# Scales of queries, keys and values: row maxima summed over the partitions by a 12-column product with ones, in place of a maximum by diagonals

## The chip, the cores and the metric

The kernel runs on one core of a Trainium2 chip. The metric is the device time of one execution in microseconds (us), on that core. Engines are named as in the profile: PE is the matrix engine, PEld its weight loads, DVE the vector engine, ACT the scalar engine, POOL the general engine, SP the engine whose queue issues the transfers. Lines such as L110 are lines of the kernel before, unless the text says that they are of the changed kernel.

## The reference

Eight batches of twelve heads with 448 positions of 64 values are put through a sigmoid attention, and its output, 3584 tokens of 768 values, through a two-layer block with an ELU between the layers:

```python
scores = scale * np.matmul(q, k.transpose(0, 1, 3, 2)) - np.log(S)
attn = 1.0 / (1.0 + np.exp(-scores))
attn_out = np.matmul(attn, v)                      # 8, 12, 448, 64
x = attn_out.transpose(0, 2, 1, 3).reshape(B * S, H * D)
h = x @ w_in                                       # 768 x 2048
g = np.where(h > 0.0, h, np.exp(np.minimum(h, 0.0)) - 1.0)
return g @ w_out                                   # 2048 x 768
```

Queries, keys, values and results are float32; the two weight matrices come as float64.

## The kernel before, in words

Products are made of two float16 parts. A tensor is multiplied by a power of two and split into a high part (written by ACT) and what is left of it (written by DVE); a product is then high by high, low by high and high by low, three PE instructions that add up in one accumulator (`split`, L120). The powers of two are made on the chip, and this is what the change is about: a scale must be the same number on all 128 partitions, and it comes from the largest absolute value of a tensor.

**Pairs of heads.** The work on attention goes by 48 pairs (eight batches `b`, six pairs `hp`). For a pair, `raw` holds queries and keys (7 tiles of 128 positions; the fourth tile has the last 64 positions of the queries in its upper 64 partitions and those of the keys in its lower 64), `rv` the values. `prepare` (L294) makes three scales for a pair: for values, queries and keys. The six pairs of batch 0 need the scale of the values alone, since their scores are made in float32 (`EXACT = 1`); the 42 pairs of batches 1 to 7 need all three. DVE takes the maximum of `rv` (L125, tile `mx`, one column) and of the seven tiles of `raw` (L125, tile `mt`, seven columns), gathers the latter to one column for queries and one for keys (L307), and adds the mixed tile to both, on 64 partitions each (two instructions of L310). Then `magnitude` (L98) finds the maximum over the partitions:

- one `dg` per scale (L105): the 128 x 128 identity times the column of maxima, a diagonal,
- one PE product of ones with these diagonals (L110, tile `pb`, 128 columns for one scale, 384 for three), which puts the maxima of all partitions side by side on every partition,
- a DVE reduction (L112, tile `al`), a lower bound (L113), and the exponent bits (L114, tile `pw`).

After that DVE and POOL make the scales `sc` from `pw` (L318 to L324, L282 to L289), ACT and DVE split `raw` into `nat` and `rv` into `vn`, and a transfer transposes `nat` into `qk` (L352).

**Steps of a pair.** `scores` (L384, accumulator `psc`) gives score tiles; `soften` makes the sigmoid (L395) and, in batches 1 to 7, splits it (`at`, L413 on ACT, L414 on DVE); `values` (L433 and L425, accumulator `pav`) multiplies with the values; `finish` splits the result into `xh`, with a running scale over the pairs (`xs`). When a batch has its six pairs, `rescale` (L443) brings all of `xh` to one scale, whose maximum again goes through `magnitude`, with one diagonal.

**The two layers.** `moe1` (L479) runs 288 products a batch (L499, accumulator `ph`) with ELU on ACT and DVE behind each 18; `moe2` (L558) runs 48 products for each of its output tiles (L529, accumulators `po` and `po_r`). An odd batch of attention has 288 products of `moe2` of the batch before to interleave, an even one 384, because the last 64 positions of two batches share a tile.

**What sets the order.** Until the end of `moe1` of batch 0 a scheduler orders the instructions by a model of their times, among them the loads and splits of the weights. From batch 1 on (L685) PE, ACT, DVE and SP run in program order: for each pair first two tiles of scores, the rest of the preparation of the next pair (`third`), five or eight products groups of `moe2` (`fill`, three products each), then the maxima and diagonals of the pair after that (`prepare_pair`), two more tiles of scores, the rest of this pair's share of `moe2`, then the product L110 with what follows it (`second`), then `values` and `finish`. So on PE the product stands between the last `po` of a pair's share and the first `pav`. The last pair of a batch keeps four groups of `moe2` back until after `finish` (`tail`).

Of the kernel before, what the change touches and what calls it, by code (L numbers as in the profile page):

```python
# [23 lines left out]
TOP = 13  # L24
ATOP = 15
TINY = 2.0**-36
WTOP = 14
XTOP = 15
GTOP = 15
# [3 lines left out]
def attention_ffn(  # L33
# [9 lines left out]
    nc = tc.nc  # L43
    B, H, S, D = q.shape
    DM, DF = w_in.shape
    P = 128
    NP = H // 2
    NC = S // P
# [37 lines left out]
    stage, w_in_words = [], []  # L86
    ones = const.tile([P, P], BF16, name="ones")
    nc.vector.memset(ones, 1.0)
    eye = const.tile([P, P], BF16, name="eye")
    nc.vector.tensor_copy(eye, ident)  # L90

    rvs = []
    for i in range(2):
# [1 line left out]
        nc.gpsimd.memset(rv[:, 2 * NC :], 0.0)  # L95
        rvs.append(rv)

    def magnitude(dst, mx, n):  # L98

        dg = sb.tile([P, n, P], BF16, tag="dg", name="dg", bufs=2)
        for i in range(n):
            nc.vector.tensor_scalar(dg[:, i], eye, mx[:, i : i + 1], None, op0=ALU.mult)  # L105

        def rest():
            pb = ps.tile([P, 512], F32, tag="pm", name="pb", bufs=3)
            row = pb[:, : n * P].rearrange("p (n x) -> p n x", x=P)
            nc.tensor.matmul(row, ones, dg, start=True, stop=True)  # L110
            al = sb.tile([P, n], F32, tag="al", name="al", bufs=2)
            nc.vector.tensor_reduce(al, row, axis=AX.X, op=ALU.max)  # L112
            nc.vector.tensor_scalar(al, al, TINY, None, op0=ALU.max)  # L113
            nc.vector.tensor_scalar(  # L114
                dst.bitcast(U32), al.bitcast(U32), 0x7F800000, None, op0=ALU.bitwise_and
            )

        return rest

# [4 lines left out]
    def absmax(dst, src):  # L124
        nc.vector.tensor_reduce(dst, src, axis=AX.X, op=ALU.max, apply_absolute_value=True)  # L125
# [151 lines left out]
    def value_scale(b, hp, pv, c, xs):  # L277


        vm, vi = xs[:, 0], xs[:, 1]  # L280
        if hp:
            nc.vector.tensor_tensor(vm[:, hp : hp + 1], vm[:, hp - 1 : hp], pv, op=ALU.max)  # L282
        else:
            nc.gpsimd.tensor_copy(vm[:, 0:1], pv)
        nc.vector.reciprocal(vi[:, hp : hp + 1], vm[:, hp : hp + 1])
        if b < EXACT:
            nc.gpsimd.tensor_scalar(c, vi[:, hp : hp + 1], 2.0 ** (XTOP - 10), None, op0=ALU.mult)
        else:
            nc.gpsimd.tensor_scalar(  # L289
                c, vi[:, hp : hp + 1], pv, 2.0 ** (XTOP - 10 - TOP - ATOP),  # L290
                op0=ALU.mult, op1=ALU.mult,
            )

    def prepare(b, hp, raw, rv, xs):  # L294


        u = f"{b}_{hp}"
        n = 1 if b < EXACT else 3
        mx = sb.tile([P, 3], F32, tag="mx", name=f"mx{u}", bufs=2)
        absmax(mx[:, 0:1], rv.rearrange("p t d -> p (t d)"))  # L300
        if n > 1:
            mt = sb.tile([P, 2, NC + 1], F32, tag="mt", name=f"mt{u}", bufs=2)
            absmax(
                mt.rearrange("p i t -> p (i t)")[:, : 2 * NC + 1],
                raw.rearrange("p t h d -> p t (h d)"),
            )
            nc.vector.tensor_reduce(mx[:, 1:3], mt[:, :, :NC], axis=AX.X, op=ALU.max)  # L307
            for i, r in enumerate(rows):
                m = mx[r, 1 + i : 2 + i]
                nc.vector.tensor_tensor(m, m, mt[r, 0, NC:], op=ALU.max)  # L310
        pw = sb.tile([P, n], F32, tag="pw", name=f"pw{u}", bufs=2)
        product = magnitude(pw, mx[:, :n], n)

        def scales():
            product()
            sc = sb.tile([P, n + 3], F32, tag="sc", name=f"sc{u}", bufs=3)
            if b >= EXACT:
                nc.vector.reciprocal(sc[:, :n], pw)  # L318
                nc.gpsimd.tensor_scalar(sc[:, :n], sc[:, :n], 2.0**TOP, None, op0=ALU.mult)

                for i, r in enumerate(rows):
                    nc.gpsimd.tensor_copy(sc[r, n + 1 : n + 2], sc[r, 1 + i : 2 + i])

                nc.gpsimd.tensor_scalar(  # L324
                    sc[:, n + 2 :], pw[:, 1:2], pw[:, 2:3], 2.0 ** (-2 * TOP) / math.sqrt(D),
                    op0=ALU.mult, op1=ALU.mult,
                )
# [36 lines left out]

        return scales
# [77 lines left out]
    def rescale(b, xh, xs):  # L443


        vm, vi, xm = xs[:, 0], xs[:, 1], xs[:, 2]
        rr = sb.tile([P, NP + 3], F32, tag="rr", name=f"rr{b}", bufs=2)
        nc.vector.tensor_scalar(rr[:, :NP], vm, vi[:, NP - 1 :], None, op0=ALU.mult)
        for c in range(NP - 1):
            nc.vector.tensor_scalar(xh[:, c], xh[:, c], rr[:, c : c + 1], None, op0=ALU.mult)  # L450
        nc.vector.tensor_tensor(
            xm[:, : NP - 1], xm[:, : NP - 1], rr[:, : NP - 1], op=ALU.mult
        )
        yield
        mx, xp, xr = (rr[:, NP + i : NP + i + 1] for i in range(3))
        nc.vector.tensor_reduce(mx, xm, axis=AX.X, op=ALU.max)
        product = magnitude(xp, mx, 1)

        def rest():
            product()  # L460
            nc.vector.reciprocal(xr, xp)

        yield xp, xr, rest

    def moe_scales(m, xs, xr):

        vm, vi = xs[:, 0, NP - 1 :], xs[:, 1, NP - 1 :]
        nc.vector.tensor_scalar(
            m[:, 0], wp, vm, 2.0 ** (10 - XTOP - WTOP), op0=ALU.mult, op1=ALU.mult
        )  # L470

        nc.vector.tensor_scalar(
            m[:, 1], wr, vi, 2.0 ** (XTOP - 10 + GTOP - 2), op0=ALU.mult, op1=ALU.mult
        )
        nc.vector.tensor_scalar(m[:, 1], m[:, 1], xr, None, op0=ALU.mult)

# [69 lines left out]
    def out_scale(b, xs, xp, i=slice(0, NH)):  # L546
        if b % 2 == 0 and i.start == 0:
            oscs[0] = sb.tile([P, 3, NH], F32, tag="osc", name=f"osc{b}", bufs=2)
        j = b % 2
        o = oscs[0][:, j, i]  # L550
        nc.gpsimd.tensor_scalar(
            o, wop[:, i], wm[:, 0:1], 2.0 ** (10 - XTOP + 2 - GTOP - WTOP),
            op0=ALU.mult, op1=ALU.mult,
        )
        nc.gpsimd.tensor_scalar(o, o, xs[:, 0, NP - 1 :], xp, op0=ALU.mult, op1=ALU.mult)
        nc.gpsimd.tensor_copy(oscs[0][rows[j], 2, i], o[rows[j]])
# [206 lines left out]
```

## Time and profile before

| what | value |
|---|---|
| median of 3 runs | 1271.27 us |
| lowest and highest of the 3 | 1269.96 and 1274.96 us |
| span of the profiled execution, first to last instruction | 1269.1 us |
| PE busy | 1200.2 us, 95% of the span |
| DVE busy | 823.4 us, 65% |
| ACT busy | 671.8 us, 53% |
| product with diagonals, L110 | 56, of which 42 with 384 columns |
| diagonals, L105 | 140 instructions |
| reductions behind the product, L112 | 56 instructions, 27.2 us |

The time of the profiled execution is not listed apart from its span; the span is 0.9 us under the lowest of the three runs and 2.2 us under their median. A view of groups gives busy time, the mean of one in ns, and the idle time ahead of the group's instructions with what ended it. A line of the timeline has the start, the time from the first start to the last end, the engine and the group; consecutive instructions of a group are merged. PE instructions are pipelined, so their rows overlap: what one takes from the engine is the distance between two starts.

### The profile page before, as it was taken

The page shows a single profiled execution, that of the slowest core. Times are in us where ns is not written, and L with a number is a line of the kernel's source. Part 1 is how long each engine was busy: PE and PEld are TensorE (multiplying, and loading weights), DVE is VectorE, ACT ScalarE, POOL GpSimd, SP SyncE. Part 2 cuts the span into 40 slices and gives each one's busy share as a digit, 9 for nine tenths or more (in the row PEclk, how much of TensorE's full clock was granted, in tenths as well). Part 3 has the DMA queues.
Part 4 walks back from the last instruction along what each step waited for, and adds up shares of the span by engine and source line. Part 5 has one row for each costly group of instructions (what it writes and reads, how often), then busy time and mean ns, then how long its engine had stood idle before and what let it go on. Part 6 is the DMA issues. An engine that isn't in the chain of part 4 may idle for free.

```text
span 1269.1 us, 19337 instructions
## 1 busy us (share of the span) xinstructions
PE 1200.2 (95%) x7246; PEld 610.5 (48%) x7246; DVE 823.4 (65%) x1872; ACT 671.8 (53%) x1015; POOL 84.1 (7%) x319
## 2 busy tenths in 40 slices
PE   5979868999999999999999999999999999999998
PEld 2324334445555554545455554545455554455565
DVE  5898989765766557775666646885576656765500
ACT  5867777643655337744555436654565435663400
POOL 0011001100000000010000000010000100100000
PEclk9889979999999999999999999999999999999999
DMA  8937423420233103340144201440034401410000
GB/s 229 281 100 222 126 77 80 100 49 1 60 84 89 37 1 83 89 86 1 37 92 92 50 1 43 105 103 7 1 86 92 92 1 22 106 43 7 1 25 26
DMA packets 213407, 89.76 MB, mean 71 GB/s; under 512 B 177472, under 2 KB 209216, under 8 KB 213312
## 3 DMA queue, kind: packets, MB, share of 16 engines
q1 hardware_dynamic: 213312, 88.51, 28.7%
q8 instruction: 57, 0.93, 0.3%
q14 instruction: 38, 0.31, 0.1%
HBM read 58.20 MB, written 11.01 MB: 55 GB/s over the span
## 4 chain that ended last, share of the span: by engine, by line
PE 78%; ACT 8%; DVE 7%; DMA 3%; issue 2%; SPq 2%; DVEq 0%; POOL 0%; ACTq 0%; POOLq 0%
PE ph L499 31%; PE po L529 25%; PE psc L384 7%; PE pav L433 6%; PE po_r L529 5%; PE pav L425 3%; ACT sg L395 2%; DMA stage<-in_moe_w_in_dram 2%; ACT at L413 1%; SPq L262 1%; PE pb L110 1%; ACT L395 1%; ACT e L511 1%; DVE e L514 1%; DMA so<-in_moe_w_out_dram 1%
## 5 line engine op out<-in xcount | busy, mean ns | idle before, releaser
L499 PE MATMUL ph<-xh,wi 128*128 128x448 f16 x2304 | 442.0, 353 | 6.1 <-DVE xh L122 2.4
L529 PE MATMUL po<-wo,g 128*128 128x384 f16 x2304 | 392.9, 328 | 0.0
L529 PEld LDWEIGHTS <-g 128*128 128x128 f16 x2688 | 257.2, 98 | 198.4 <-issue 36.3
L499 PEld LDWEIGHTS <-wi 128*128 128x128 f16 x2304 | 225.3, 98 | 218.4 <-issue 7.6
L511 ACT ACTIVATE e<-ph,msc 128x448 f32<-128x448 f32 x128 | 80.8, 633 | 211.7 <-PE ph L499 211.6
L414 DVE SCALAR_TENSOR_TENSOR at<-sg,at 128x896 f16<-128x896 f32 x126 | 137.2, 1090 | 84.5 <-ACT at L413 84.5
L395 ACT ACTIVATE sg<-psc,bias,sc 128x896 f32<-128x896 f32 (+1 forms) x168 | 166.6, 992 | 1.7
L513 DVE TENSOR_SCALAR e<-e 128x448 f32<-128x448 f32 x128 | 50.3, 394 | 170.8 <-ACT e L511 170.7
L121 ACT ACTIVATE xh<-pav,sc 128x448 f16<-128x448 f32 x48 | 30.3, 632 | 216.7 <-PE pav L425 216.7
L384 PE MATMUL psc<-qk 64*128 64x448 f16 x1008 | 116.6, 355 | 11.4 <-ACT sg L395 11.4
L413 ACT ACTIVATE at<-sg 128x896 f16<-128x896 f32 x126 | 119.8, 951 | 4.1
L121 ACT ACTIVATE g<-e,msc 128x384 f16<-128x384 f32 (+1 forms) x192 | 96.0, 534 | 6.0 <-DVE e L514 4.3
L122 DVE SCALAR_TENSOR_TENSOR g<-e,msc,g 128x384 f16<-128x384 f32 (+1 forms) x192 | 94.6, 521 | 0.6
L514 DVE SCALAR_TENSOR_TENSOR e<-ph,msc,e 128x448 f32<-128x448 f32 x128 | 87.3, 683 | 4.0
L384 PEld LDWEIGHTS <-qk 64*128 64x128 f16 x1008 | 41.7, 97 | 89.7 <-issue 60.2
L433 PE MATMUL pav<-at,vn 128*64 128x448 f16 x756 | 80.2, 357 | 0.0
L324 POOL TENSOR_SCALAR sc<-pw 128x1 f32<-128x1 f32 x42 | 12.4, 295 | 843.5 <-DVE pw L114 790.9
L529 PE MATMUL po_r<-wo,g 128*128 128x384 f16 x384 | 64.7, 326 | 0.0
L122 DVE SCALAR_TENSOR_TENSOR xh<-pav,sc,xh 128x448 f16<-128x448 f32 x48 | 32.7, 680 | 48.7 <-ACT xh L121 48.7
L433 PEld LDWEIGHTS <-vn 128*64 128x64 f16 x756 | 39.4, 110 | 50.0 <-issue 27.8
L122 DVE SCALAR_TENSOR_TENSOR nat<-raw,sc,nat 128x384 f16<-128x384 f32 (+1 forms) x126 | 59.1, 524 | 0.0
L121 ACT ACTIVATE nat<-raw,sc 128x384 f16<-128x384 f32 (+1 forms) x126 | 58.8, 529 | 0.0
(103 smaller groups left out, 852.7 us busy)
## 6 DMA issues: line engine op xcount, KB each, us to landing
stage<-in_moe_w_in_dram SPq DMA_DIRECT2D x16, 768.0 KB, 6.6
raw<-in_q_dram SPq DMA_DIRECT2D x96, 96.0 KB, 3.1
raw<-in_k_dram SPq DMA_DIRECT2D x96, 96.0 KB, 2.6
rv<-in_v_dram SPq DMA_DIRECT2D x48, 192.0 KB, 2.7
out_dram<-o SPq DMA_DIRECT2D x48, 192.0 KB, 2.1
wo<-in_moe_w_out_dram SPq DMA_DIRECT2D x19, 384.0 KB, 4.1
so<-in_moe_w_out_dram SPq DMA_DIRECT2D x13, 384.0 KB, 4.3
raw<-in_q_dram SPq DMA_DIRECT2D x48, 32.0 KB, 2.4
```

Of the source, the lines that this page charges most:

```text
L121: nc.scalar.mul(hi, src, s)
L122: nc.vector.scalar_tensor_tensor(lo, src, s, hi, op0=ALU.mult, op1=ALU.subtract)
L384: nc.tensor.matmul(psc[:, j, :S] if g < NC else psc[rows[j], 0, :S], kk[rows[j], o], qq[rows[j], :S], start=(n == 0), stop=(n == len(parts ...
L395: a = nc.scalar.activation(sg[:, :nb], psc[:, :nb, :S], AF.Sigmoid, bias=bias, scale=self.s_scale)
L413: nc.scalar.mul(hi, sg, 2.0**ATOP)
L414: nc.vector.scalar_tensor_tensor(lo, sg, 2.0**ATOP, hi, op0=ALU.mult, op1=ALU.subtract)
L433: nc.tensor.matmul(pav[rows[j], :S], vv[i][:, j * NC + g], sg[k][:, j], start=(g == 0 and n == 0), stop=False,)
L499: nc.tensor.matmul(ph[:, :S], wi[:, wj, c, f * P : (f + 1) * P], xh[:, c, xj], start=(n == 0), stop=(n == 3 * NK - 1),)
L511: a = nc.scalar.activation(e, ph[:, :S], AF.Exp, scale=inv)
L513: nc.vector.tensor_scalar(e, e, 1.0, -1.0, op0=ALU.min, op1=ALU.add)
L514: nc.vector.scalar_tensor_tensor(e, ph[:, :S], inv, e, op0=ALU.mult, op1=ALU.max)
L529: nc.tensor.matmul(po[:, :HM], lh(gj, f), wo[:, i, f, wj], start=(n == 0), stop=(n == 3 * NF - 1),)
```

## The change

Instead of finding the maximum over the partitions, the kernel adds up over the partitions. DVE now writes maxima in bfloat16 into one tile `mx` of 15 columns, three groups of four with a gap: four for the values (`rv` is cut in four), three tiles each for queries and keys, and the mixed tile's maximum in both groups' last column, multiplied by a column that is one on its half of the partitions and zero on the other (`half`). PE multiplies ones with the 12 columns themselves (4 in batch 0), which puts the sum over the partitions of each column on every partition; DVE takes the largest of each four. The sum is an upper bound of the maximum, up to 128 times as large, so the constant for the running scale changes from 2^-10 to 2^-3 (`XBITS`). The maximum of `rescale` is still found by one diagonal, now made from the float32 identity (`greatest`); the bfloat16 copy of the identity is gone.

```diff
+    half = const.tile([P, 2], BF16, name="half")
+    nc.vector.memset(half, 0.0)
+    nc.vector.memset(half[:R, 0:1], 1.0)
+    nc.vector.memset(half[R:, 1:2], 1.0)
...
-    def magnitude(dst, mx, n):
-        dg = sb.tile([P, n, P], BF16, tag="dg", name="dg", bufs=2)
-        for i in range(n):
-            nc.vector.tensor_scalar(dg[:, i], eye, mx[:, i : i + 1], None, op0=ALU.mult)
+    def greatest(dst, mx):
+        dg = sb.tile([P, P], BF16, tag="dg", name="dg")
+        nc.vector.tensor_scalar(dg, ident, mx, None, op0=ALU.mult)
...
+    def sums_of_rows(dst, mx):
+        n = mx.shape[1]
         def rest():
-            pb = ps.tile([P, 512], F32, tag="pm", name="pb", bufs=3)
-            row = pb[:, : n * P].rearrange("p (n x) -> p n x", x=P)
-            nc.tensor.matmul(row, ones, dg, start=True, stop=True)
+            pb = ps.tile([P, 512], F32, tag="pm", name="pr", bufs=3)
+            sums = pb[:, : 4 * n].rearrange("p (n x) -> p n x", x=4)
+            nc.tensor.matmul(sums, ones, mx, start=True, stop=True)
             al = sb.tile([P, n], F32, tag="al", name="al", bufs=2)
-            nc.vector.tensor_reduce(al, row, axis=AX.X, op=ALU.max)
+            nc.vector.tensor_reduce(al, sums, axis=AX.X, op=ALU.max)
+            power_of_two(dst, al, TINY)
...
-        mx = sb.tile([P, 3], F32, tag="mx", name=f"mx{u}", bufs=2)
-        absmax(mx[:, 0:1], rv.rearrange("p t d -> p (t d)"))
+        mx = sb.tile([P, 15], BF16, tag="mx", name=f"mx{u}", bufs=2)
+        groups = mx.rearrange("p (n x) -> p n x", x=5)[:, :n, :4]
+        absmax(mx[:, 0:4], rv.rearrange("p (a t) d -> p a (t d)", a=4))
         if n > 1:
-            mt = sb.tile([P, 2, NC + 1], F32, tag="mt", name=f"mt{u}", bufs=2)
-            absmax(
-                mt.rearrange("p i t -> p (i t)")[:, : 2 * NC + 1],
-                raw.rearrange("p t h d -> p t (h d)"),
-            )
-            nc.vector.tensor_reduce(mx[:, 1:3], mt[:, :, :NC], axis=AX.X, op=ALU.max)
-            for i, r in enumerate(rows):
-                m = mx[r, 1 + i : 2 + i]
-                nc.vector.tensor_tensor(m, m, mt[r, 0, NC:], op=ALU.max)
+            absmax(mx[:, 6 : 2 * NC + 7], raw.rearrange("p t h d -> p t (h d)"))
+            nc.vector.tensor_tensor(
+                mx[:, 5:14:8], mx[:, 9:10].to_broadcast([P, 2]), half, op=ALU.mult
+            )
...
-            nc.gpsimd.tensor_scalar(c, vi[:, hp : hp + 1], 2.0 ** (XTOP - 10), None, op0=ALU.mult)
+            nc.gpsimd.tensor_scalar(c, vi[:, hp : hp + 1], 2.0 ** (XTOP - XBITS), None, op0=ALU.mult)
...
-        product = magnitude(xp, mx, 1)
+        product = greatest(xp, mx)
```

The order of the instructions shows three places. The first is DVE during pair 4 of batch 1, between the split of the next pair's values (`vn`) and the reduction behind the product; the digits in a name are the pair's number and a count. Before:

```order
L122 SCALAR_TENSOR_TENSOR vn_5_2351<-rv_85,sc_5_2286,vn_5_2351 128x384
L125 TENSOR_REDUCE mx_0_2384<-rv_83 128x1
L125 TENSOR_REDUCE mt_0_2386<-raw_0_2185 128x7
L307 TENSOR_REDUCE mx_0_2384<-mt_0_2386 128x2
L310 TENSOR_TENSOR mx_0_2384<-mx_0_2384,mt_0_2386 64x1 x2
L105 TENSOR_SCALAR dg<-eye,mx_0_2384 128x128 x3
L414 SCALAR_TENSOR_TENSOR at_4_2405<-sg_4_2403,at_4_2405 128x896
L537 TENSOR_SCALAR o_1_1_2450<-po_1_1_2366,osc_1613 128x384
L112 TENSOR_REDUCE al<-pb 128x3
```

And DVE at the same place of the changed kernel:

```order
L138 SCALAR_TENSOR_TENSOR vn_5_2299<-rv_87,sc_5_2234,vn_5_2299 128x384
L141 TENSOR_REDUCE mx_0_2332<-rv_85 128x4
L141 TENSOR_REDUCE mx_0_2332<-raw_0_2140 128x7
L321 TENSOR_TENSOR mx_0_2332<-mx_0_2332,half 128x2
L427 SCALAR_TENSOR_TENSOR at_4_2346<-sg_4_2344,at_4_2346 128x896
L550 TENSOR_SCALAR o_1_1_2391<-po_1_1_2314,osc_1589 128x384
L131 TENSOR_REDUCE al<-pr 128x3
```

Six instructions (L307, two of L310, three of L105) have become one (L321); the rest stands in the same order. The second place is PE where the product stands in the same pair, between `moe2` and `values`. Before:

```order
L529 LDWEIGHTS g
L529 MATMUL po_1_1_2366<-wo,g 128x384
L110 LDWEIGHTS ones
L110 MATMUL pb<-dg,ones 128x384
L433 LDWEIGHTS vn_4_2180
L433 MATMUL pav_4_2468<-at_4_2327,vn_4_2180 64x448
```

And PE in the changed kernel:

```order
L542 LDWEIGHTS g
L542 MATMUL po_1_1_2314<-wo,g 128x384
L129 LDWEIGHTS ones
L129 MATMUL pr<-mx_0_2332,ones 128x12
L446 LDWEIGHTS vn_4_2135
L446 MATMUL pav_4_2409<-at_4_2275,vn_4_2135 64x448
```

The product has 12 columns instead of 384 and stands at the same place. The third place is SP's queue in the part that the scheduler orders, around the loads of pair 0 of batch 1 (`raw_0`) and the loads of the first weight matrix (`stage`). Before:

```order
L266 DMA raw_5_521<-in_k_dram 64x2x64
L181 DMA stage<-in_moe_w_in_dram 128x6x128
L247 DMA rv_83<-in_v_dram 128x2x192
L262 DMA raw_0_649<-in_q_dram 128x3x64 x2
L252 DMA rv_83<-in_v_dram 64x64 x2
L266 DMA raw_0_649<-in_q_dram 64x2x64
L262 DMA raw_0_649<-in_k_dram 128x3x64 x2
L266 DMA raw_0_649<-in_k_dram 64x2x64
L181 DMA stage<-in_moe_w_in_dram 128x6x128 x3
```

And SP's queue in the changed kernel:

```order
L282 DMA raw_5_515<-in_k_dram 64x2x64
L197 DMA stage<-in_moe_w_in_dram 128x6x128 x3
L263 DMA rv_85<-in_v_dram 128x2x192
L278 DMA raw_0_641<-in_q_dram 128x3x64 x2
L282 DMA raw_0_641<-in_q_dram 64x2x64
L268 DMA rv_85<-in_v_dram 64x64 x2
L197 DMA stage<-in_moe_w_in_dram 128x6x128
L278 DMA raw_0_641<-in_k_dram 128x3x64 x2
L197 DMA stage<-in_moe_w_in_dram 128x6x128
L282 DMA raw_0_641<-in_k_dram 64x2x64
```

The loads of the weights have moved among the loads of queries, keys and values, some ahead and some back by a few places; PE, ACT and DVE are likewise reordered in the part that ends with `moe1` of batch 0 and the rest of the work on the second weight matrix: of that work ACT has 54 of 64 conversions and 12 of 32 splits ahead of its change from exponentials to sigmoids (at 162.9 us in the profile) before, and 58 and 16 now. From about 190 us on, the order differs only where instructions are gone or replaced.

More of the change, by code (lines that the diff above doesn't have):

```diff
@@ L26 @@
 TINY = 2.0**-36
+XTINY = 2.0**-24
+XBITS = 3
 WTOP = 14
@@ L88, in attention_ffn @@
     nc.vector.memset(ones, 1.0)
-    eye = const.tile([P, P], BF16, name="eye")
-    nc.vector.tensor_copy(eye, ident)
+    half = const.tile([P, 2], BF16, name="half")
+    nc.vector.memset(half, 0.0)
+    nc.vector.memset(half[:R, 0:1], 1.0)
+    nc.vector.memset(half[R:, 1:2], 1.0)
     rvs = []
@@ L96, in attention_ffn, with power_of_two, rest @@
         rvs.append(rv)
-    def magnitude(dst, mx, n):
-        dg = sb.tile([P, n, P], BF16, tag="dg", name="dg", bufs=2)
-        for i in range(n):
-            nc.vector.tensor_scalar(dg[:, i], eye, mx[:, i : i + 1], None, op0=ALU.mult)
+    def power_of_two(dst, al, tiny):
+        nc.vector.tensor_scalar(al, al, tiny, None, op0=ALU.max)
+        nc.vector.tensor_scalar(
+            dst.bitcast(U32), al.bitcast(U32), 0x7F800000, None, op0=ALU.bitwise_and
+        )
+    def greatest(dst, mx):
+        dg = sb.tile([P, P], BF16, tag="dg", name="dg")
+        nc.vector.tensor_scalar(dg, ident, mx, None, op0=ALU.mult)
         def rest():
             pb = ps.tile([P, 512], F32, tag="pm", name="pb", bufs=3)
-            row = pb[:, : n * P].rearrange("p (n x) -> p n x", x=P)
-            nc.tensor.matmul(row, ones, dg, start=True, stop=True)
-            al = sb.tile([P, n], F32, tag="al", name="al", bufs=2)
[L112 to L115, printed above, removed]
-            )
+            nc.tensor.matmul(pb[:, :P], ones, dg, start=True, stop=True)
+            al = sb.tile([P, 1], F32, tag="al", name="al", bufs=2)
+            nc.vector.tensor_reduce(al, pb[:, :P], axis=AX.X, op=ALU.max)
+            power_of_two(dst, al, XTINY)
+        return rest
+    def sums_of_rows(dst, mx):
+        n = mx.shape[1]
+        def rest():
+            pb = ps.tile([P, 512], F32, tag="pm", name="pr", bufs=3)
+            sums = pb[:, : 4 * n].rearrange("p (n x) -> p n x", x=4)
+            nc.tensor.matmul(sums, ones, mx, start=True, stop=True)
+            al = sb.tile([P, n], F32, tag="al", name="al", bufs=2)
+            nc.vector.tensor_reduce(al, sums, axis=AX.X, op=ALU.max)
+            power_of_two(dst, al, TINY)
         return rest
@@ L286, in value_scale @@
         if b < EXACT:
-            nc.gpsimd.tensor_scalar(c, vi[:, hp : hp + 1], 2.0 ** (XTOP - 10), None, op0=ALU.mult)
+            nc.gpsimd.tensor_scalar(c, vi[:, hp : hp + 1], 2.0 ** (XTOP - XBITS), None, op0=ALU.mult)
         else:
             nc.gpsimd.tensor_scalar(
-                c, vi[:, hp : hp + 1], pv, 2.0 ** (XTOP - 10 - TOP - ATOP),
+                c, vi[:, hp : hp + 1], pv, 2.0 ** (XTOP - XBITS - TOP - ATOP),
                 op0=ALU.mult, op1=ALU.mult,
@@ L298, in prepare @@
         n = 1 if b < EXACT else 3
-        mx = sb.tile([P, 3], F32, tag="mx", name=f"mx{u}", bufs=2)
-        absmax(mx[:, 0:1], rv.rearrange("p t d -> p (t d)"))
+        mx = sb.tile([P, 15], BF16, tag="mx", name=f"mx{u}", bufs=2)
+        groups = mx.rearrange("p (n x) -> p n x", x=5)[:, :n, :4]
+        absmax(mx[:, 0:4], rv.rearrange("p (a t) d -> p a (t d)", a=4))
         if n > 1:
-            mt = sb.tile([P, 2, NC + 1], F32, tag="mt", name=f"mt{u}", bufs=2)
-            absmax(
-                mt.rearrange("p i t -> p (i t)")[:, : 2 * NC + 1],
-                raw.rearrange("p t h d -> p t (h d)"),
-            )
-            nc.vector.tensor_reduce(mx[:, 1:3], mt[:, :, :NC], axis=AX.X, op=ALU.max)
-            for i, r in enumerate(rows):
-                m = mx[r, 1 + i : 2 + i]
-                nc.vector.tensor_tensor(m, m, mt[r, 0, NC:], op=ALU.max)
+            absmax(mx[:, 6 : 2 * NC + 7], raw.rearrange("p t h d -> p t (h d)"))
+            nc.vector.tensor_tensor(
+                mx[:, 5:14:8], mx[:, 9:10].to_broadcast([P, 2]), half, op=ALU.mult
+            )
         pw = sb.tile([P, n], F32, tag="pw", name=f"pw{u}", bufs=2)
-        product = magnitude(pw, mx[:, :n], n)
+        product = sums_of_rows(pw, groups)
         def scales():
@@ L468, in moe_scales @@
         nc.vector.tensor_scalar(
-            m[:, 0], wp, vm, 2.0 ** (10 - XTOP - WTOP), op0=ALU.mult, op1=ALU.mult
+            m[:, 0], wp, vm, 2.0 ** (XBITS - XTOP - WTOP), op0=ALU.mult, op1=ALU.mult
         )
         nc.vector.tensor_scalar(
-            m[:, 1], wr, vi, 2.0 ** (XTOP - 10 + GTOP - 2), op0=ALU.mult, op1=ALU.mult
+            m[:, 1], wr, vi, 2.0 ** (XTOP - XBITS + GTOP - 2), op0=ALU.mult, op1=ALU.mult
         )
@@ L551, in out_scale @@
         nc.gpsimd.tensor_scalar(
-            o, wop[:, i], wm[:, 0:1], 2.0 ** (10 - XTOP + 2 - GTOP - WTOP),
+            o, wop[:, i], wm[:, 0:1], 2.0 ** (XBITS - XTOP + 2 - GTOP - WTOP),
             op0=ALU.mult, op1=ALU.mult,
```

## The prediction

> **What bounds the kernel now.** I read the page's busy times first, then the busy times by stretch (below: stretch, its length, busy time of PE, PEld, DVE, ACT and POOL, PE clock, DMA share, GB/s), then PE's waits, and last the timeline around a few of the products that change.
>
> ```profile
> span 1269.1 us, 19337 instructions
> PE 1200.2 (95%) x7246; PEld 610.5 (48%) x7246; DVE 823.4 (65%) x1872; ACT 671.8 (53%) x1015; POOL 84.1 (7%) x319
> ...
> 0.00:60.00 60.00, 42.96 (x209) 17.84 (x211) 42.70 (x97) 40.12 (x52) 3.72 (x19) 0.94 0.91 249
> 60.00:153.00 93.00, 78.20 (x406) 35.70 (x405) 84.90 (x220) 66.34 (x113) 10.91 (x30) 0.96 0.50 153
> 153.00:200.00 47.00, 32.68 (x169) 15.07 (x169) 40.18 (x84) 38.02 (x65) 4.89 (x12) 0.80 0.31 88
> 200.00:1269.10 1069.10, 1046.32 (x6467) 541.89 (x6464) 655.60 (x1475) 527.33 (x788) 64.56 (x259) 1.00 0.24 53
> ```
>
> There are two kernels in one. Up to 60 us the DMA engines are 0.91 busy; from 60 to 200 us DVE leads (84.9 of 93, then 40.2 of 47 us). From 200 us on PE is busy for all but 22.8 us, and DVE for only 61%. So in the long part only two things count: time that a product takes on PE, and PE's waits. The latter are few:
>
> ```profile
> PE pb L110 <- DVE dg L105: 11.6, 6, 2.0
> PE psc L384 <- ACT sg L395: 6.7, 6, 1.2
> ```
>
> The largest wait from 200 us on is the very product that changes, six times for diagonals that DVE has not finished. One of the six, where an odd batch begins:
>
> ```profile
> 484.43 1.08 DVE L125 TENSOR_REDUCE mt<-raw 128x7 f32<-128x896 f32 x1
> ...
> 485.55 0.16 DVE L307 TENSOR_REDUCE mx<-mt 128x2 f32<-128x6 f32 x1
> 485.74 0.34 DVE L310 TENSOR_TENSOR mx<-mx,mt 64x1 f32<-64x1 f32 x2
> 486.11 0.58 DVE L105 TENSOR_SCALAR dg<-eye,mx 128x128 bf16<-128x128 bf16 x3
> 486.61 1.08 DVE L414 SCALAR_TENSOR_TENSOR at<-sg,at 128x896 f16<-128x896 f32 x1
> 486.75 0.32 PE L110 MATMUL pb<-dg,ones 128*128 128x384 bf16 x1 [1.97 <-DVE dg L105]
> ...
> 487.00 1.89 PE L433 MATMUL pav<-at,vn 128*64 128x448 f16 x18
> ```
>
> DVE runs without a break from the maxima to the diagonals, and PE starts 0.06 us after the third. PE stood still for 1.97 us; nothing else held it.
>
> **The change part by part.** The rows for what is removed, and for its nearest relatives:
>
> ```profile
> L125 DVE TENSOR_REDUCE mt<-raw 128x7 f32<-128x896 f32 x42 | 45.2, 1076 | 0.0
> L125 DVE TENSOR_REDUCE mx<-rv 128x1 f32<-128x512 f32 x48 | 32.6, 679 | 0.6 <-DMA rv<-in_v_dram 0.5 <-issue 0.2
> ...
> L105 DVE TENSOR_SCALAR dg<-eye,mx 128x128 bf16<-128x128 bf16 x132 | 26.1, 251 | 1.4
> L112 DVE TENSOR_REDUCE al<-pb 128x3 f32<-128x384 f32 x42 | 23.2, 551 | 15.2 <-PE pb L110 15.2
> L310 DVE TENSOR_TENSOR mx<-mx,mt 64x1 f32<-64x1 f32 x84 | 12.9, 154 | 2.7
> L307 DVE TENSOR_REDUCE mx<-mt 128x2 f32<-128x6 f32 x42 | 6.7, 159 | 1.3
> L112 DVE TENSOR_REDUCE al<-pb 128x1 f32<-128x128 f32 x14 | 4.0, 288 | 16.8 <-PE pb L110 16.8
> ```
>
> *The long waits.* From the start of L307 to the product it is 486.75 - 485.55 = 1.20 us. In its place stands one small instruction, 0.16 us by L307 and L310, and the same 0.06 us to PE: 0.22 us. So the product starts 0.98 us earlier, and six times that is 5.9 us. The two maxima ahead keep their price: their rows differ by 397 ns over 384 elements, about one ns an element, with seven results or with one, so I give nothing for four results instead of one. Were they slower by 0.1 us each, 1.2 us of the 5.9 would go; the other end is 11.6 us, were the waits to vanish. They will not: 1.97 - 0.98 leaves 0.99 us, because the chain ahead (sigmoid, split, `nat`, `vn`, the maxima) is not shortened. Behind the product PE needs the `at` of L414 only for its 17th and 18th `pav`; at 1.89 us for 18 these come some 1.6 us in, while that `at`, next in DVE's queue, ends within 1.1 us of the column. So no new wait appears there.
>
> *The short waits.* In odd batches most other products also stand behind their diagonals, for a moment that the view of waits does not show, since a product's row reaches into the next one's:
>
> ```profile
> 219.02 0.81 PE L529 MATMUL po<-wo,g 128*128 128x384 f16 x4
> 219.78 0.32 PE L110 MATMUL pb<-dg,ones 128*128 128x384 bf16 x1
> 220.03 0.38 PE L433 MATMUL pav<-at,vn 128*64 128x448 f16 x2
> ...
> 365.68 0.98 PE L529 MATMUL po_r<-wo,g 128*128 128x384 f16 x5
> 366.49 0.33 PE L110 MATMUL pb<-dg,ones 128*128 128x384 bf16 x1
> 366.75 0.57 PE L433 MATMUL pav<-at,vn 128*64 128x448 f16 x4
> ...
> 1117.11 0.81 PE L529 MATMUL po<-wo,g 128*128 128x384 f16 x4
> 1117.88 0.32 PE L110 MATMUL pb<-dg,ones 128*128 128x384 bf16 x1
> ```
>
> At 366.49 the product starts 0.17 us before the row of the `po` ends (366.66), at 219.78 only 0.05 us before (219.83): 0.12 us lost. From 219.78 to 1117.88 us, the first and the last shown, there are 14 such products; with a column that is ready 0.98 us earlier none should be left: 14 x 0.12 = 1.7 us.
>
> *The product itself.* What it takes from PE is the distance to the first `pav`: 0.26 us at 366.49, 0.25 us at 219.78. A product of 128 columns ahead of a `pav` is there once:
>
> ```profile
> 17.97 0.22 PE L110 MATMUL pb<-dg,ones 128*128 128x128 bf16 x1
> 18.11 0.60 PE L433 MATMUL pav<-sg,rv 128*64 128x448 f32 x2
> ```
>
> That is 0.14 us. So 256 columns cost 0.11 us, 0.43 ns each, and at 12 columns 0.14 - 116 x 0.43 ns = 0.09 us are left, which are the turn to the half-width weights of `pav` and stay. Saved: 0.16 us. How many there are, the reductions behind them (L112) say, of which 7 from 200 us on belong to `rescale`:
>
> ```profile
> 200.00:1269.10 1069.10, 23.55 (x46) 1.00 0.24 53
> ```
>
> So 39 of the 42 products lie behind 200 us: 39 x 0.16 = 6.2 us. This extrapolates below any row, so I bound it. At best all 0.16 us go; at worst a short product cannot follow its neighbours closer than the closest products with weights of their own do here:
>
> ```profile
> 52.30 0.51 PE L150 MATMUL si<-stage,ones 128*128 128x128 bf16 x6 [0.31 <-DVE al L112]
> ```
>
> Five distances and one row of 0.22 us make 0.51 us: 58 ns. Then the product takes 0.06 + 0.09 = 0.15 us and saves 0.10 us, 3.9 us in all. I take the upper value, since 58 ns is what 128 columns need at 0.43 ns (55 ns) and so shows no floor. [...]
>
> *The rest of DVE.* The reduction behind the product falls from 551 ns to 551 - 372 x 1.03 = 168 ns (slope from the two L112 rows), the three diagonals go, three small instructions become one: 0.75 + 0.38 + 0.31 = 1.4 us a pair. From 200 us on this beyond the waits is worth nothing: DVE is idle there for 39% of the time, and the scales behind it have time until `third`, on PE behind 18 `pav` (1.89 us above) and two tiles of scores. The diagonal of `rescale` reads float32 now; eight instructions, with the second layer's first products to hide them.
>
> *The start.* From 60 to 200 us DVE spends 2.7 us on diagonals:
>
> ```profile
> 60.00:200.00 140.00, 2.70 (x12) 0.91 0.44 131
> ```
>
> With three products of three scales in it (0.38 + 0.31 us each) and two or three small ones, some 4.8 us of DVE's work go where DVE is 89% busy. At most all of it is gained. Against it stands the scheduler's new order, in which loads of the first weights trade places with those of queries and keys; a load lands after 6.6 us:
>
> ```profile
> stage<-in_moe_w_in_dram SPq DMA_DIRECT2D x16, 768.0 KB, 6.6
> ```
>
> One such load late on the path costs up to 6.6 us. Between 4.8 gained and 6.6 lost I take half the relief, 2.4 us, since the first loads stand where they stood and the last ones end at the same place in the queue.
>
> **Sum.** 5.9 + 1.7 + 6.2 + 2.4 = 16.2 us: the span goes from 1269.1 to 1252.9 us. The median shown lies 2.2 us above the profiled span, so 1255.1 us, about 1255.
>
> **The rivals.**
> *A floor under short products:* the product saves 0.10 us, not 0.16: 2.3 us less, 1257.4 us. For it speaks that no row has so few columns. [...]
> *The waits stay:* the long waits do not shrink, because maxima into bfloat16 columns are dearer or the new instruction, which reads what was written just before it, starts late: 5.9 us less, and the short waits too: 1255.1 + 7.6 = 1262.7 us. Against it: L307 started 0.04 us after `mt` ended, in the same position.
> *The start eats it:* one load late costs 6.6 us instead of the 2.4 gained: 1255.1 + 9.0 = 1264.1 us.
> *Slower:* the same mechanism at its full size, the scheduler's order setting the first weights back. It decides once the start loses more than the 13.8 us of the steady part: three loads one behind the other, 3 x 6.6 = 19.8 us, 1271.27 - 13.8 + 19.8 = 1277 us. The queue's new order shows no load moved that far.
> *It does not do what it says:* the product might still be of many columns, or more instructions; the order shows one of 12. If only waits were saved: 1255.1 + 6.2 = 1261.3 us.
>
> **How the numbers follow.** The forecast has 0.60, the floor 0.13, waits that stay 0.08, a start that eats it 0.11, slower 0.03, no shorter product 0.05. The range: from 1249 (all 4.8 us of the start and 3 to 4 us more of the long waits) to 1264, where the start has eaten its part. The kernel's runs can tell some 0.5%, 6.4 us, from no change, so faster means under 1264.9 us: 0.89 with most of the cases above, the same 0.08 for a start that loses more than one load, slower 0.03.
>
> **What would show it.** The start is read by the last exponential of batch 0 and the change of tables behind it:
>
> ```profile
> 162.22 0.64 ACT e L511
> 162.87 1.28 ACT L395
> ```
> Right: PE's wait for DVE at the product is six times about 1.0 us (5.7 us in all) on the new column; the product to the first `pav` takes about 0.09 us; the odd batches' other products follow their `po` at 0.16 us; PE's busy time from 200 us on is down by 6 us. Wrong: waits of PE on ACT that were not there, a distance of 0.15 us or more at the product, or a last exponential of batch 0 that comes later than 162.2 us. The forecast as a whole fails if, from 200 us on, an odd batch does not shrink by some 3.4 us (6 x 0.16 + 2 x 0.98 + 4 x 0.12) and an even one by 1.0 us (6 x 0.16).

## The result, and the profile after

The changed kernel takes 1253.16 us, median of 4 runs (1252.55 to 1255.70), against 1273.05 us for the kernel before (4 runs, 1269.96 to 1274.96): a ratio on record of 0.9855, with a 95% interval of 0.9834 to 0.9875 (the quotient of the two medians, 0.984, lies in it). The forecast was 1255, the range 1249 to 1264. The profiled execution of the changed kernel spans 1253.8 us, 15.3 us less than that of the kernel before.

The page's head and the busy time by stretch, as shown before (stretch, its length, busy time of PE, PEld, DVE, ACT and POOL, PE clock, DMA share, GB/s):

```profile
span 1253.8 us, 19128 instructions
PE 1190.9 (95%) x7246; PEld 610.0 (49%) x7246; DVE 771.3 (62%) x1658; ACT 672.6 (54%) x1015; POOL 87.7 (7%) x319
...
0.00:60.00 60.00, 44.69 (x211) 17.88 (x211) 39.43 (x97) 41.32 (x53) 5.87 (x22) 0.94 0.94 253
60.00:153.00 93.00, 77.73 (x401) 35.70 (x398) 84.77 (x206) 66.97 (x115) 12.71 (x27) 0.94 0.53 156
153.00:200.00 47.00, 31.57 (x175) 14.96 (x174) 38.55 (x78) 37.24 (x62) 4.65 (x12) 0.87 0.28 79
200.00:1253.80 1053.80, 1036.92 (x6467) 541.49 (x6465) 608.58 (x1280) 527.05 (x788) 64.44 (x258) 1.00 0.24 54
```

DVE has 52 us less to do, of which 5.0 us lie before 200 us (167.8 and 162.8 us). PE's busy time from 200 us on is down by 9.4 us, more than the 6 us of the forecast; what makes up the rest is told behind the experiments. PE's waits from 200 us on:

```profile
PE psc L397 <- ACT sg L408: 6.8, 6, 1.2
PE pr L129 <- DVE mx L321: 5.8, 6, 1.0
```

The same six waits are there, with half their length: 5.8 us instead of 11.6. The one that the prediction showed, in the timeline:

```profile
481.24 1.08 DVE L141 TENSOR_REDUCE mx<-raw 128x7 bf16<-128x896 f32 x1
482.35 0.17 DVE L321 TENSOR_TENSOR mx<-mx,half 128x2 bf16<-128x2 bf16 x1
482.43 1.08 DVE L427 SCALAR_TENSOR_TENSOR at<-sg,at 128x896 f16<-128x896 f32 x1
482.57 0.17 PE L129 MATMUL pr<-mx,ones 128*128 128x12 bf16 x1 [0.99 <-DVE mx L321]
482.67 1.51 PE L446 MATMUL pav<-at,vn 128*64 128x448 f16 x14
```

From the start of L321 to the product it is 0.22 us, where it was 1.20 us. The other two places: the first of the odd batches' products that stood behind their diagonals for a moment (219.34 us), and the product of an even batch (363.92 us).

```profile
218.36 1.14 PE L542 MATMUL po<-wo,g 128*128 128x384 f16 x6
219.34 0.17 PE L129 MATMUL pr<-mx,ones 128*128 128x12 bf16 x1
219.44 0.57 PE L446 MATMUL pav<-at,vn 128*64 128x448 f16 x4
...
363.92 0.17 PE L129 MATMUL pr<-mx,ones 128*128 128x12 bf16 x1
364.02 0.57 PE L446 MATMUL pav<-at,vn 128*64 128x448 f16 x4
```

From the product to the first `pav` it is 0.10 us at both, and at 219.34 us the product starts 0.16 us before the row of the `po` ends (219.50): nothing holds it any more. The DVE groups:

```profile
L141 DVE TENSOR_REDUCE mx<-raw 128x7 bf16<-128x896 f32 x42 | 45.3, 1079 | 0.0
L141 DVE TENSOR_REDUCE mx<-rv 128x4 bf16<-128x512 f32 x48 | 32.6, 679 | 3.3 <-DMA rv<-in_v_dram 3.1
...
L321 DVE TENSOR_TENSOR mx<-mx,half 128x2 bf16<-128x2 bf16 x42 | 7.1, 169 | 1.3
L131 DVE TENSOR_REDUCE al<-pr 128x3 f32<-128x12 f32 x42 | 6.9, 164 | 24.3 <-PE pr L129 24.1
```

The maxima cost the same with four results and in bfloat16 (679 and 1079 ns against 679 and 1076), the new instruction 169 ns, the reduction behind the product 164 ns against 551.

### The profile page after: what moved, and what is told of

It is laid out like the page before. It is cut to its first block, busy times and chain, and to the rows that moved or that the text cites. A ratio compares the mean times of both kernels' runs of the same rounds, so it can differ in the third digit from the quotient of the medians.

```text
span 1253.8 us, 19128 instructions
## 1 busy us (share of the span) xinstructions
PE 1190.9 (95%) x7246; PEld 610.0 (49%) x7246; DVE 771.3 (62%) x1658; ACT 672.6 (54%) x1015; POOL 87.7 (7%) x319
## 4 chain that ended last, share of the span: by engine, by line
PE 78%; DVE 7%; ACT 7%; DMA 5%; issue 2%; SPq 1%; DVEq 0%; POOL 0%; ACTq 0%
PE ph L512 30%; PE po L542 25%; PE psc L397 7%; PE pav L446 7%; PE po_r L542 5%; PE pav L438 3%; DMA stage<-in_moe_w_in_dram 3%; ACT sg L408 2%; ACT at L426 1%; DVE mx L141 1%; DMA wo<-in_moe_w_out_dram 1%; ACT L408 1%; DVE wo L173 1%; DVE wo L159 1%; ACT e L524 1%
## 5 line engine op out<-in xcount | busy, mean ns | idle before, releaser
L446 PEld LDWEIGHTS <-vn 128*64 128x64 f16 x756 | 39.2, 109 | 36.2 <-issue 13.9
```

The lines of the kernel that those rows point to most:

```text
L446: nc.tensor.matmul(pav[rows[j], :S], vv[i][:, j * NC + g], sg[k][:, j], start=(g == 0 and n == 0), stop=False,)
```

## The experiments

All times are medians. Each kernel was timed in turn with the kernel before on one chip, and the ratio is to that. The first four rows were timed together, so their last column compares like with like; further down the last column, but for the two spreads, is against a time from another chip, and the ratios are the better measure there. The changed kernel itself is the yardstick.

| run | median us | ratio to before, 95% interval | against the changed kernel's 1253.13 |
|---|---|---|---|
| changed kernel, again | 1253.13 | 0.985 (0.9825 to 0.9874) | |
| 384 columns again | 1259.29 | 0.990 (0.9871 to 0.9928) | +6.2 |
| DVE time put back | 1262.34 | 0.9921 (0.9895 to 0.9947) | +9.2 |
| old start | 1258.16 | 0.9882 (0.9859 to 0.9905) | +5.0 |
| second spread, new start / old start | 1255.04 / 1260.85 | 0.9858 / 0.9902 | 5.8 between the two |
| third spread, new start / old start | 1253.13 / 1258.89 | 0.9841 / 0.9888 | 5.8 between the two |
| twice the DVE time (one run) | 1290.38 | | +37.3 |
| other shares | 1249.93 | 0.9825 (0.9802 to 0.9848) | -3.2 |
| product behind the values | 1248.50 | 0.9818 (0.9789 to 0.9847) | -4.6 |
| the same, maxima behind the split | 1247.26 | 0.9799 (0.9781 to 0.9818) | -5.9 |

**The yardstick.** No edit.

> The changed kernel again, as the yardstick for the others on the same chip. Both theories: 0.9855 of the kernel before, six waits at the product of 0.92 to 1.00 us each, 0.10 us from the product to the first pav, and no fall of the PE clock between 202 us and the last microseconds.

It came out as expected: 0.985, waits of 5.8 us in six, and a full clock from 203 us to the last microsecond.

**The columns alone.** From pair 8 on the twelve columns are repeated until there are 384; nothing else changes, and the order of all engines is that of the changed kernel.

```diff
-            nc.tensor.matmul(sums, ones, mx, start=True, stop=True)
+            if wide:
+                nc.tensor.matmul(
+                    pb[:, : 32 * 4 * n].rearrange("p (r n x) -> p r n x", r=32, x=4), ones,
+                    mx.unsqueeze(1).to_broadcast([P, 32, n, 4]), start=True, stop=True,
+                )
+            else:
+                nc.tensor.matmul(sums, ones, mx, start=True, stop=True)
...
+        product = sums_of_rows(pw, groups, b * NP + hp >= (EXACT + 0) * NP + 2)
```

> The changed kernel with 384 columns in each of the 40 products from pair 8 on (the twelve columns repeated 32 times; the sums are the same, the reduction still reads twelve). The order of all engines is that of the changed kernel. Theory, each column costs PE 0.42 ns and nothing covers it: the product to the first pav goes back from 0.10 to 0.25 us, 39 x 0.155 = 6.0 us more than the changed kernel (ratio to before 0.990 instead of 0.9855), and the six waits stay at 0.9 to 1.0 us each. Rival, the columns were covered by something else and the gain came from DVE alone: within 1.5 us of the changed kernel.

It took 6.2 us more. The timeline at the same product as above, then PE's wait at it:

```profile
361.49 0.35 PE L130 MATMUL pr<-mx,ones 128*128 128x384 bf16 x1
361.78 0.57 PE L452 MATMUL pav<-at,vn 128*64 128x448 f16 x4
...
PE pr L130 <- DVE mx L327: 5.7, 6, 1.0
```

The distance is 0.29 us, where it was 0.26 us with the diagonals at this place (366.49 us in the kernel before) and is 0.10 us with twelve columns. This operand is read in three nested steps of which one does not advance; whether the added 0.03 us come from that was not tested. The waits are as in the changed kernel. From the end of batch 1 to that of batch 2 (the change of ACT's tables, at 265.34 and 418.20 us) this run takes 152.86 us, the changed kernel 151.78 us: 0.18 us for each of six products. So the columns were on the path: 0.18 - 0.03 = 0.15 us a product, some 6 us for 39 of them, by themselves.

**The DVE chain alone.** From pair 8 on, what DVE no longer does is put back ahead of the new instruction, into tiles that nobody reads (the six instructions alone are shown).

```diff
+        nc.vector.tensor_reduce(dmr[:, 1:3], dmy[:, :, :NC], axis=AX.X, op=ALU.max)
+        for i, r in enumerate(rows):
+            m = dmr[r, 1 + i : 2 + i]
+            nc.vector.tensor_tensor(m, m, dmy[r, 0, NC:], op=ALU.max)
+        for i in range(3):
+            nc.vector.tensor_scalar(dmg[:, i], ones, bias, None, op0=ALU.mult)
```

> The changed kernel with the DVE time put back ahead of the product: from pair 8 on one small reduction, two small tensor-tensor instructions and three 128-column products by a scalar, into tiles that nothing reads, stand between the maxima and the new instruction. The product keeps its twelve columns. Theory, PE waits for the end of a DVE chain: the six waits go back from 0.92-1.00 to about 2.0 us each (6 x 1.1 = 6.6 us), 14 products of odd batches are held by about 0.2 us again (2.6 us at most), 8 to 9 us more than the changed kernel; a fall of the PE clock behind one of the long waits can add 1.6 us each. The reductions behind the product stay short. Rival, the waits of PE are set by ACT and the diagonals only ended last by chance: under 2 us more.

It took 9.2 us more. PE's waits and one of the six places:

```profile
PE pr L142 <- DVE mx L336: 11.1, 6, 1.9
...
480.39 0.58 DVE L107 TENSOR_SCALAR dmg<-ones,bias 128x128 bf16<-128x128 bf16 x3
480.88 0.16 DVE L336 TENSOR_TENSOR mx<-mx,half 128x2 bf16<-128x2 bf16 x1
...
481.10 0.17 PE L142 MATMUL pr<-mx,ones 128*128 128x12 bf16 x1 [1.87 <-DVE mx L336]
```

The chain is 0.88 us longer, not 1.0, and the waits grow by that: 11.1 - 5.8 = 5.3 us. The short waits came back only as some 0.03 us each, 0.4 us for 14 of them, and not as the 0.2 us expected. Besides, the PE clock fell three times in this execution, at 1.6 us each (below): batch 3, which holds two long waits and one fall, takes 141.67 us instead of 138.24 us, and 2 x 0.88 + 4 x 0.03 + 1.60 = 3.48 us are near those 3.43 us. Together this is 10.5 us, 1.3 us more than the medians differ by; that is within what the start varies by (next experiment). DVE's chain sets the waits; ACT does not.

**The start.** Up to pair 7 the maxima go by diagonals again, in the order of the kernel before on every engine (the spare tile `half` is filled by POOL, and a factor of 128 in an instruction that is there anyway makes the scales fit); from pair 8 on it is the changed kernel.

```diff
+        if b * NP + hp < EXACT * NP + 2:
+            mx = sb.tile([P, 3], F32, tag="mx", name=f"mx{u}", bufs=2)
...
+            return scales_of(magnitude(pw, mx[:, :n], n, 128.0), pw, b, hp, u, n, raw, rv, xs)
...
-        product = greatest(xp, mx)
+        product = magnitude(xp, mx, 1, 1.0)
```

> The kernel before up to pair 7 (maxima by diagonals, its order of all engines in the start, word for word), the changed kernel from pair 8 on; the scales of the first eight pairs are multiplied by 128 in an instruction that is there anyway, so that both kinds of scales fit. Theory, the start gained nothing (the product at 187 us came 0.2 us earlier): within 1 us of the changed kernel. Rival, as forecast: the relief of DVE in the start is worth 2.4 us, so this is 2.4 us slower than the changed kernel. Second rival: the scheduler's new order cost something that the relief paid for; then this is slower or faster by as much as the first products of batch 1 are later or earlier than at 186.9 us.

It is 5.0 us slower than the changed kernel, so the start does gain, more than the forecast's 2.4 us, and my theory at this point, taken from the two profiles (first product of batch 1 at 187.07 and 186.85 us), fell. The change of ACT's tables at the end of the attention of batches 1 and 7, first of this kernel, then of the changed one:

```profile
270.74 1.28 ACT L550 ACT_TABLE_LOAD   x1 [5.85 <-DVE msc L507]
1139.69 1.28 ACT L550 ACT_TABLE_LOAD   x1 [5.85 <-DVE msc L507]
...
268.12 1.28 ACT L524 ACT_TABLE_LOAD   x1 [5.85 <-DVE msc L481]
1137.07 1.28 ACT L524 ACT_TABLE_LOAD   x1 [5.85 <-DVE msc L481]
```

Between the two it is 868.95 us in both: all of the difference lies ahead. But the start is not the same in every execution. With one and the same order of the start, that first change of tables stood at 268.12 and 268.29 us in the two profiles of the changed kernel, and at 265.34 and 265.77 us in those of the kernels with 384 columns and with the DVE time put back, though these have more to do ahead of it. A start can't be judged by one profile each; the timed runs do it: the four times of the old start lie from 1256.43 to 1258.33 us, the yardstick's from 1252.51 to 1255.76 us.

**The start, luck of the order or less work?** The scheduler orders the start anew when its instructions change, so the 5.0 us could be the order's. Two other spreads of the first weights' tiles make it order anew once more, each with the new and the old start. The second is shown; the third is [1, 2, 5, 8, 11, 14, 16].

```diff
-    W_IN = [1, 3, 6, 9, 12, 15, 16]
+    W_IN = [1, 4, 7, 10, 13, 15, 16]
```

> The changed kernel with another spread of the first weights' tiles over the pairs of batch 0 (up to 1, 4, 7, 10, 13, 15, 16 instead of 1, 3, 6, 9, 12, 15, 16), which makes the scheduler order the start anew. To be compared with the same spread on the old start. Theory, the start gains because DVE has 4.8 us less to do: new start 3 to 6 us faster than the old one at this spread too. Rival, the 5.0 us between the old and the new start were the luck of the scheduler's order: the difference at this spread is anything between -3 and 3 us.

> The old start (maxima by diagonals up to pair 7) with the same other spread, the changed kernel from pair 8 on. Theory: 3 to 6 us slower than the new start at this spread. Rival: within 3 us of it on either side.

> The changed kernel with a third spread (up to 1, 2, 5, 8, 11, 14, 16). Same question: theory, 3 to 6 us faster than the old start at this spread; rival, any difference between -3 and 3 us.

> The old start with the third spread. Theory: 3 to 6 us slower than the new start at this spread. Rival: within 3 us of it on either side.

5.8 us at both spreads, after 5.0 us. With three orders of each kind the new start is faster by much the same, while the spreads among themselves differ by 0 to 2.7 us. The gain goes with the lighter work and not with one lucky order. How it divides between DVE's lighter work (5.0 us less by the profiles) and PE's shorter products was not separated.

**The clock.** The chain ahead of the product is lengthened by twice as much (`range(2)` around the six instructions above).

> The changed kernel with twice the DVE time of the experiment before put ahead of the product (chain longer by 1.8 us instead of 0.9). By the waits alone: 6 x 1.8 us, 13 products of odd batches with 0.91 us to spare held for 0.9 us, the first product of each even batch for 0.45 us: 24 us more than the changed kernel, some 1277 us. Theory on the clock, a stretch of 3.4 us in which PE stands still for some 2 us or more is followed by one at half clock: the long waits are now 2.7 to 2.8 us, and half clock follows most of the six, 1.6 us each, so 1283 to 1287 us. Rival, the fall behind a wait of 1.97 us in the kernel before was chance: none or one.

The one run took 1290.4 us, over the 1283 to 1287 us expected. PE's wait at the product is 31.1 us in 23 places, 25.3 us more than in the changed kernel; the clock fell four times between 203 us and the last microseconds. In 17 of the 23 places PE had no wait before, and the product started 0.16 us ahead of the end of the row before it; these 17 x 0.16 = 2.7 us are lost too and do not show as waits. With 4 x 1.6 us for the clock that makes 34.4 us, against 34.7 us between the spans of the two profiles (1288.5 and 1253.8 us). So most of it is waits, and some is the clock.

What a fall costs shows in the kernel before: its batch 5 holds one and takes 143.16 us from change of tables to change of tables (717.38 to 860.54 us), its batch 3 holds none and takes 141.56 us. That is 1.60 us. What decides whether the clock falls shows in the busy times of stretches of 3.4 us: in the kernel before around 782 us (it fell) and around the same place two batches earlier (it did not), then in the run with the DVE time put back where it fell, and last in the same run where it did not.

```profile
778.90:782.30 3.40, 1.43 (x14) 0.65 (x14) 3.27 (x9) 0.72 (x2) 0.00 (x0) 1.00 0.88 174
782.30:785.70 3.40, 3.40 (x14) 1.02 (x12) 1.38 (x7) 0.00 (x0) 1.12 (x5) 0.50 0.57 127
...
482.00:485.40 3.40, 2.77 (x18) 1.56 (x16) 3.40 (x7) 3.31 (x5) 0.00 (x0) 1.00 0.22 44
485.40:488.80 3.40, 2.06 (x19) 0.93 (x18) 3.23 (x11) 0.00 (x0) 0.00 (x0) 1.00 0.78 158
...
478.92:482.33 3.41, 1.54 (x15) 0.79 (x15) 3.35 (x11) 0.86 (x2) 0.00 (x0) 1.00 0.88 171
482.33:485.74 3.41, 3.41 (x13) 1.00 (x10) 1.04 (x7) 0.22 (x1) 1.27 (x6) 0.50 0.55 126
...
253.65:257.06 3.41, 1.60 (x15) 0.82 (x14) 3.35 (x10) 1.34 (x2) 0.00 (x0) 1.00 0.90 148
257.06:260.47 3.41, 3.41 (x25) 1.77 (x22) 3.24 (x15) 0.63 (x1) 0.33 (x2) 1.00 0.53 119
```

PE's busy time is the first number behind each length; the clock is the third column from the right. The clock is halved in the stretch behind one with PE busy for 1.43 or 1.54 us. It is not behind one with 1.60 us, nor where the same wait of 1.97 us was cut in two (2.77 and 2.06 us). In the kernel before the clock changes at 198.63, 202.04, 782.31 and 785.72 us: 1, 170 and 1 times 3.41 us apart. PE did not stand still for the whole of the stretch ahead of a fall: 1.97 and 1.87 us of it were enough in the two falls shown. All fourteen profiles, cut into such stretches at the points where the clock changes, agree: the clock never fell behind a stretch with PE busy for more than 1.75 us (at most 1.7 us in the kernel before and 1.5 us in the changed one), and stayed up only once behind one with less than 1.55 us (1.45 us, at 92.8 us of the kernel before). In these profiles the limit lies near half of the stretch, between 1.45 and 1.75 us.

**Can the last waits go?** First by the second layer's products: two more groups ahead of the products that wait, one less ahead of each of the others.

```diff
                 share = left // (NP - hp)
+                if b % 2 and b > EXACT:
+                    share = [18, 15, 15, 15, 15, 18][hp]
+                elif b % 2:
+                    share = [16, 16, 16, 15, 15, 18][hp]
```

> The changed kernel with the second layer's products shared out differently in odd batches: 18, 15, 15, 15, 15, 18 groups of three products over the six pairs instead of 16 each (16, 16, 16, 15, 15, 18 in batch 1). The two pairs that wait get two groups more ahead of their product, 6 x 0.16 = 0.98 us, the others lose one of 0.49 us, of which they have 0.91 us to spare. Theory, the remaining waits of 0.92 to 1.00 us are DVE's chain against PE's share of work: all six go, 5.8 us less than the changed kernel, about 1247.5 us. Rival, the waits go where the share went: the four pairs in between wait as much, and the time is within 1.5 us of the changed kernel.

3.2 us faster, between theory and rival. PE's waits, and two products of the last pairs of batch 3:

```profile
PE pr L129 <- DVE mx L321: 1.4, 3, 0.5
...
532.71 0.17 PE L129 MATMUL pr<-mx,ones 128*128 128x12 bf16 x1
...
545.76 0.17 PE L129 MATMUL pr<-mx,ones 128*128 128x12 bf16 x1 [0.47 <-DVE mx L321]
```

The waits where odd batches begin are gone, those where they end are half. The products stand 13.05 us apart here, and 13.06 us in batch 1 (243.98 and 257.04 us). My reading is that the chain through ACT and DVE takes 13.05 us a pair, so that the product can't start sooner when a pair is given less; that was not tested by itself.

Second, the product and its reduction behind the values products, in the six pairs alone (`held`):

```diff
-                third = second()
+                if not held:
+                    third = second()
                 for t in range(NC + 1):
                     p.values(t)
+                if held:
+                    third = second()
```

> The changed kernel with the product and the reduction behind it put after the values products in the six pairs that wait; PE has 18 + 2 products in its place, 2.8 us, more than the wait. Theory: the six waits go, 5.8 us less than the changed kernel, as with the new shares. Rival: the scales come 2.8 us later, the split of queries and keys by ACT waits for them, and the next pair's first scores or product start later; then less than 3 us are gained or nothing.

4.6 us faster, short of the 5.8 us of the theory. The waits at the product are gone, and six new ones have come at the values:

```profile
PE pav L446 <- DVE at L427: 1.9, 6, 0.4
```

The split of the third tile stands behind the maxima in DVE's queue, and now PE gets there sooner. So, third, in the same six pairs the maxima go behind that split:

```diff
-                second = prepare_pair(n + 2)
+                if not held:
+                    second = prepare_pair(n + 2)
                 for t in range(2, NC + 1):
                     p.scores(t)
                     p.soften(t)
+                    if held and t == 2:
+                        second = prepare_pair(n + 2)
```

> The experiment that put the product behind the values in the six pairs that wait left 0.32 us at each, now of the values products for the split of the third tile (L427), which stands behind the maxima in DVE's queue. Here, in the same six pairs, the maxima stand behind that split. Theory, both waits are the same DVE chain and its order decides who is late: waits of PE on DVE from 200 us on of under 0.7 us in all (0.1 us each), 5.3 to 5.8 us less than the changed kernel, 1247.3 to 1247.8 us. Rival, DVE idles until ACT has written the high part of that tile and the product then comes too late for the next pair's scales: waits come back at the product or at the scores, and nothing is gained over the experiment before (1248.5 us).

1247.26 us, and of PE's waits from 200 us on only one group is left:

```profile
PE psc L397 <- ACT sg L408: 6.7, 6, 1.2
```

This version beats both kernels: 0.9799 of the kernel before (0.9781 to 0.9818, the changed kernel 0.9825 to 0.9874), 5.9 us under the changed one. How the three versions rank is shown less well, because the start varies. From the change of tables at the end of batch 1 to that of batch 7, which the start does not touch, the changed kernel takes 868.95 us, the other shares 865.40 us (266.50 to 1131.90), the product behind the values 865.92 us (262.93 to 1128.85) and the last version 864.73 us (264.19 to 1128.92). The last is the fastest by this too; the first two are not told apart.

## Why the prediction was right, and where a step was off

- *The long waits.* 0.98 us each, 5.9 us in all, were forecast; 11.6 - 5.8 = 5.8 us were measured, and the run with the chain put back shows the cause. That about 0.99 us would be left, and no new wait appear behind 200 us, held too (PE's waits for ACT are 6.8 us, 6.7 us before).
- *The short waits.* 14 x 0.12 = 1.7 us were forecast. The products follow their `po` at 0.16 us now, and the shrinking of the odd batches (below) leaves 0.11 us for each of the four.
- *The product.* 0.16 us each from 0.09 us left, 6.2 us in all; measured 0.10 us left, so 0.15 to 0.16 us. The run with 384 columns bears it out batch by batch: 0.18 us a product, of which 0.03 us are what these 384 columns take over those of the diagonals (0.29 against 0.26 us). The rival with a floor of 58 ns under short products falls. A row that the prediction did not have shows a distance below it:

```profile
86.93 0.17 PE L129 MATMUL pr<-mx,ones 128*128 128x12 bf16 x1
86.96 0.51 PE L166 MATMUL si<-stage,ones 128*128 128x128 bf16 x6
```

  Twelve columns, followed by a product with the same full width: 0.03 us. The other 0.07 us of the 0.10 us come where half-width weights follow; what in this turn takes the time was not tested.
- *The batches.* An odd batch was to shrink by 3.4 us and an even one by 1.0 us. The change of tables at the end of batches 2, 3 and 4, before and after:

```profile
423.10 1.28 ACT L511 ACT_TABLE_LOAD   x1 [5.85 <-DVE msc L468]
564.66 1.28 ACT L511 ACT_TABLE_LOAD   x1 [5.85 <-DVE msc L468]
717.38 1.28 ACT L511 ACT_TABLE_LOAD   x1 [5.85 <-DVE msc L468]
...
419.90 1.28 ACT L524 ACT_TABLE_LOAD   x1 [5.85 <-DVE msc L481]
558.14 1.28 ACT L524 ACT_TABLE_LOAD   x1 [5.85 <-DVE msc L481]
709.92 1.28 ACT L524 ACT_TABLE_LOAD   x1 [5.85 <-DVE msc L481]
```

  Batch 3 shrank from 141.56 to 138.24 us, by 3.3 us; batch 4 from 152.72 to 151.78 us, by 0.9 us. The clock stayed up in both, so this is the mechanism alone.
- *The start.* This is the term that was mis-sized: half of DVE's relief, 2.4 us, was taken, against a rival in which the start eats it; it gains 5.0 to 5.8 us, all of the relief and more than the 4.8 us that were its upper end. The sign that the prediction named, a last exponential later than 162.2 us, misled: the change of tables right behind it came at 165.5 us instead of 162.9 us while the start as a whole was no slower. It moves from one execution to the next: with the same order of the start it stood at 161.94 us in the run with 384 columns and at 162.47 us in the last version.
- *What was not in the sum.* The fall of the clock behind a long wait, 1.6 us at 782 us in the profile before, and none in that after. It is a part of why PE's busy time fell by 9.4 and not 6 us. Another part is a slip of the sign itself: the short waits lie within PE's rows, so their 1.7 us count as busy time that goes, beside the products' 6.2 us.
- *The total.* The two profiles differ by 15.3 us, all of it behind 200 us, where 6467 products are left in both: 13.7 us beside the 1.6 us of the clock, against 13.8 us in the sum, and nothing of the start. The medians show the start: of the 18.9 us between the kernel before (1272.04 us) and the changed kernel timed with it, 13.9 us are left with the old start, and 5.0 us are the start's. How much of the 13.9 us is the clock in the timed runs stays open. The 19.9 us between the first medians are 3.7 us more than the 16.2 us forecast. The time itself missed by 2 us only, and that is in part luck: the forecast started from 1271.27 us, and the kernel before came out at 1273.05 us.

## What to carry to other kernels

Where one engine is busy all the time, ask of a small instruction in its stream two things: its distance to the next one, which is its price (here 0.26 us with 384 columns, 0.10 us with twelve), and what it waits for (here a chain of DVE, for 1.97 us and then for 0.99 us). A maximum that only needs to be a bound can be had as a sum, and a product with ones makes it from a dozen columns instead of some hundred. A wait that the change had halved went away here when the waiting instruction was put behind work that is ready, but only once DVE's queue had that work first.

## What the runs showed of the hardware that I had not expected

The clock of PE fell to one half for 3.41 us behind a stretch of that length in which PE was busy for less than about half (1.43 and 1.54 us at the falls shown). So a wait of 1.97 us came to 1.97 + 1.60 = 3.57 us in batch 5 of the kernel before, and to 1.97 us alone in batch 3, where it was cut in two by the stretches. This may be one reason why executions of one kernel differ by some us: fourteen runs of the kernel before, on two chips, took from 1268.95 us, with a mean granted clock of 0.989, to 1275.91 us, with 0.981. That it explains all of the difference was not shown.
